# Half blocks of a head pair scored in one matmul, and whole-block scores moved beside the values, in an attention + two-MLP kernel

## Chip, cores and metric

The kernel runs on one core of a Trainium2 chip. The metric is the device time of one execution in microseconds, the median of the runs shown. The profile is of one further execution, whose own time is given beside its span.

## What is computed

The reference is windowed attention with a linear position bias (window 128), followed by two MLPs over the 2304 tokens. Sequences have 576 rows, that is four whole blocks of 128 and a half block of 64.

```python
# B, H, S, D = 4, 8, 576, 64
scores = scale * np.matmul(q, k.transpose(0, 1, 3, 2))
...
mask = (rel >= 0) & (rel < window)
scores = np.where(mask, scores + bias[None], -1000000000.0)
...
attn = np.exp(scores)
attn = attn / (np.sum(attn, axis=-1, keepdims=True) + 1e-09)
return np.matmul(attn, v).astype(np.float32)
...
h = x @ w_in                       # first MLP: 512 -> 2048 -> 512
relu6 = np.clip(h + 3.0, 0.0, 6.0)
return ((h * relu6 / 6.0) @ w_out).astype(np.float32)
...
r = np.maximum(x @ w_in, 0.0)      # second MLP
return ((s * (r * r) + b) @ w_out).astype(np.float32)
```

## The kernel before

**Groups and heads.** Attention is cut into eight groups: rows 0 to 255 of each of the four sequences (groups 0 to 3), then rows 256 to 575 of each (groups 4 to 7, two whole blocks and the half block). Groups 0 and 1 are `StartUnit`s and nothing of them moves. Groups 2 to 7 are `Unit`s, one per head, planned in pairs of an even and an odd head: 24 pairs, 16 of them with half blocks. A pair's two heads lie on partitions 0 to 63 and 64 to 127 of one `raw` tile.

**One pair's work.** `load` fetches queries and keys, `scale` (ACT, L330) scales the queries, `scores` (PE, L345) multiplies a block of 128 queries with 64 rows of contraction by 256 keys (192 for the half block), `minima` (DVE, L358 and L359) picks the right half of the two key blocks with a mask and takes each row's minimum while it writes P, `exps` (ACT, L369) takes the exponential and its sum, `sums` (DVE, L376 and L379) inverts the sum, `weights` (POOL, L385) multiplies P by it, `transposes` (PE, L394) turns P, `fold` (ACT, L398), `lower` (DVE, L407) and `masks` (POOL, L419) spread it over its two key blocks, `values` (PE, L434) multiplies by the values into 64 output columns per head, and `to_hi` and `to_lo` (ACT L445, DVE L449) split the result into two parts for the MLP.

**The first MLP** runs beside it. Per tile of tokens and per 128 hidden columns f, `h` (L609) makes 12 matmuls into one PSUM bank, ACT takes the relu (L620), DVE the product (L623, it frees that bank), ACT and DVE split it (L630, L634), and `o` (L647) makes 12 matmuls. Token tiles are 256 wide for groups 0 to 3 and 320 wide for groups 4 to 7. DVE, ACT and POOL also split the second MLP's weights (class `Pair`, L723 to L809), and the second MLP follows at the end (L999 and L1059).

**Order.** Nothing is scheduled by the compiler: `at(slot, rank, fn)` fills a table, and slots are emitted in order, within a slot by rank. For token tiles 2 to 6 an odd slot holds one `o` and one `h`; the attention matmuls stand in the even slots between. A pair begins at an odd slot s, and the next pair at s + 8. Before, its PE work stands at s+1 (half scores of both heads, right behind the `values` of the pair two before it), s+3 (whole scores, behind the even head's transposes of the pair before it) and, for its own transposes and values, s+11, s+13 and s+17. From the second token tile on, scores, transposes and values share three PSUM banks, which come free in the order in which the program releases them. SP issues all DMAs in program order.

Of the kernel before, what the change touches and what calls it, by code (L numbers as in the profile page):

```python
# [8 lines left out]
F32 = mybir.dt.float32  # L9
# [14 lines left out]
def tile_alibi_window_attention_moe_moe2(  # L24
# [87 lines left out]
    s_sb, b_sb, b2_sb = (scalar[:, i : i + 1] for i in range(3))  # L112

    def constants():
        tmp = xpool.tile([P, P], F32, tag="s0", name="tmp")
# [21 lines left out]
        for h in range(H):  # L137
            c = -(D ** -0.5) / slopes[h]
            nc.gpsimd.memset(qscale[h % 2 * D : (h % 2 + 1) * D, h // 2 : h // 2 + 1], c)

    def scalars():
# [121 lines left out]
    class Unit:  # L263


        def __init__(self, g, b, qa, qb, h):
            self.g, self.b, self.qa, self.qb, self.h = g, b, qa, qb, h
            self.ka = max(0, qa - 1)
            self.nq = min(qb * P, S) - qa * P
            self.nk = min(qb * P, S) - self.ka * P  # L270
            self.nkb = qb - self.ka
            self.id = f"{b}_{qa}_{h}"
            self.Pt = None

        def plan(self, s):
            two = min(self.qa + 2, self.qb)
            odd = self.h % 2
            s -= 4 * odd
            if not odd:
# [24 lines left out]
        def load(self):  # L304
            i, b = (1, self.b) if self.qa else (0, self.b - NATIVE)
            n = (self.qb - self.qa) * P
            raw = ap.tile([P, 832], F32, tag="raw", name=f"raw{self.id}")[:, : n + self.nk]
            if self.nq < n:
                nc.gpsimd.memset(raw[:, self.nq : n], 0.0)
            for u in self.pair():  # L310
                u.p = slice((u.h % 2) * D, (u.h % 2 + 1) * D)
# [3 lines left out]
                u.q = raw[:, : self.nq]  # L315
                u.X = raw[u.p, :n]
                u.rk = raw[u.p, n:]
                u.ps = []

# [12 lines left out]
        def square(self, i):  # L332
            o = (i - self.qa) % 2 * 256
            k0 = max(0, i - 1) * P
            k1 = min((i + 1) * P, S)
            return self.ps[-1 if i < self.qa + 2 else 0][:, o : o + k1 - k0], k0, k1

        def scores(self, a, b):
            for u in self.pair():
                u.ps.append(bank(f"s{u.id}_{a}")) if a < b else None  # L340
            for i in range(a, b):
                for u in self.pair():
# [6 lines left out]

        def minima(self, a, b):  # L350
            if self.Pt is None:
                self.Pt = ap.tile([P, 3, P], F32, tag="P", bufs=5, name=f"P{self.id}")
                self.st = ap.tile([P, 3, 3], F32, tag="st", bufs=6, name=f"st{self.id}")
            for i in range(a, b):
                sl = self.square(i)[0]
                li, r = i - self.qa, rows(i)
                if i:
                    nc.vector.copy_predicated(out=sl[:, :r], mask=own[:, :r], data=sl[:, P:])  # L358
                nc.vector.tensor_tensor_reduce(  # L359
                    out=self.Pt[:, li], in0=sl[:, :P], in1=rel if i else rel0,  # L360
                    scale=slopes[self.h], scalar=3.0e38, op0=ALU.add, op1=ALU.min,
                    accum_out=self.st[:, 0, li : li + 1],
                )

        def exps(self, a, b):
            for i in range(a, b):
                li = i - self.qa
                pt = self.Pt[:, li]
                nc.scalar.activation(  # L369
                    pt, pt, AF.Exp, bias=self.st[:, 0, li : li + 1], scale=-1.0,  # L370
                    accum_out=self.st[:, 1, li : li + 1],
                )

        def sums(self):
            n, st = self.qb - self.qa, self.st
            nc.vector.tensor_scalar(  # L376
                out=st[:, 2, :n], in0=st[:, 1, :n], scalar1=1e-9, scalar2=None, op0=ALU.add
            )
            nc.vector.reciprocal(st[:, 2, :n], st[:, 2, :n])  # L379

        def weights(self):
            for i in range(self.qa, self.qb):
                li = i - self.qa
                pt = self.Pt[:, li]
                nc.gpsimd.tensor_scalar(  # L385
                    out=pt, in0=pt, scalar1=self.st[:, 2, li : li + 1], scalar2=1.0,
                    op0=ALU.mult, op1=ALU.mult,
                )

        def transposes(self):  # L390
            self.pt = bank(f"t{self.id}")
            for i in range(self.qa, self.qb):
                li = i - self.qa
                nc.tensor.transpose(self.pt[:, li * P : (li + 1) * P], self.Pt[:, li], ident)  # L394

        def fold(self):
            self.F = ap.tile([P, 320], F32, tag="F", bufs=1, name=f"F{self.id}")[:, : self.nq]
            nc.scalar.activation(self.F, self.pt[:, : self.nq], AF.Copy)  # L398

# [11 lines left out]
        def masks(self):  # L411
            for i in range(self.qa, self.qb):
                q, r = (i - self.qa) * P, rows(i)
                for k in (0, 1):
                    if (i == 0, i - self.qa < 2)[k]:
                        continue
                    o = 2 * q + k * r
                    s = 1 if k else -1
                    nc.gpsimd.affine_select(  # L419
                        out=self.W[:, o : o + r], in_=self.F[:, q : q + r], fill=0.0,  # L420
                        base=k - 1, compare_op=ALU.is_ge, pattern=[[s, r]], channel_multiplier=-s,
                    )

# [29 lines left out]
    class StartUnit(Unit):  # L453
# [66 lines left out]
        def minima(self):  # L520
            self.Pt = ap.tile([P, 3 * P], F32, tag="P", bufs=5, name=f"P{self.id}")
            self.st = ap.tile([P, 3, 3], F32, tag="st", bufs=6, name=f"st{self.id}")
            for i, a, b in self.blocks:
# [681 lines left out]
    for i in range(FIRST):  # L1205
        at(i, 20.7, lambda i=i: warm_up(4 if i < 4 else 2))
    at(-3, 0, constants)
    at(hslot[1, NF - 1], 1, scalars)

# [59 lines left out]
```

## Time and profile before

| | us |
|---|---|
| median of 3 runs | 922.55 (922.35 to 925.35) |
| the profiled execution | 922.92 |
| its span, first to last instruction | 921.2 |

| stretch of the span, us | what runs |
|---|---|
| 0 to 60 | start, groups 0 and 1 of attention |
| 60 to 190 | token tiles 0 to 2 of the first MLP; attention of groups 2 and 3 |
| 190 to 490 | token tiles 2 to 6; attention of groups 4 to 7 |
| 490 to 562 | the rest of the first MLP |
| 562 to 921 | second MLP |

The profile lists per engine what ran and what ended an idle time. A merged row of the order of time gives the start of the first instruction, the busy time of the run and its count. Matmuls overlap in the pipeline, so the time that a run of them takes is read from its start to the start of the next run, and a plain matmul of float32 operands is two instructions.

### The profile page before, as it was taken

How to read it: one execution, taken by the hardware profiler on the slowest of the kernel's cores; microseconds unless marked ns; L12 is line 12 of the kernel's file. 1: busy time of each engine (PE TensorE's matmuls, PEld its weight loads, DVE VectorE, ACT ScalarE, POOL GpSimd, SP SyncE). 2: the span in 40 equal slices, each digit the busy share in tenths (PEclk: the TensorE clock that was granted, in tenths of full speed). 3: DMA queues.
4: the chain of work that ended last, by engine and by line, in shares of the span. 5: the costliest groups of instructions: out<-in, count | busy, mean ns of one | idle time of the engine just before them, and what ended most of it. 6: DMA issues, size and time to landing. Idle time of an engine off the chain costs nothing.

```text
span 921.2 us, 17887 instructions
## 1 busy us (share of the span) xinstructions
PE 893.6 (97%) x6517; PEld 840.8 (91%) x6517; DVE 650.1 (71%) x1472; ACT 526.6 (57%) x1259; POOL 350.1 (38%) x518
## 2 busy tenths in 40 slices
PE   9898899999999999999999999999999999999998
PEld 4588789888988998999899999999999999999997
DVE  7899885666787777677766744778747787566662
ACT  7877775455655655565554534665626665266550
POOL 7834451333554463446443410444004450144200
PEclk9999999999999999999999999999999999999999
DMA  9344332517356436543635362977778787777872
GB/s 341 130 154 132 110 103 88 182 36 221 140 189 214 160 122 208 191 156 114 228 135 194 123 271 82 330 274 276 267 252 309 260 307 249 260 254 261 282 269 75
DMA packets 63944, 183.10 MB, mean 199 GB/s; under 512 B 7152, under 2 KB 26736, under 8 KB 55408
## 3 DMA queue, kind: packets, MB, share of 16 engines
q1 hardware_dynamic: 63856, 181.95, 57.6%
q8 instruction: 52, 0.85, 0.4%
q14 instruction: 36, 0.29, 0.1%
HBM read 143.13 MB, written 38.80 MB: 197 GB/s over the span
## 4 chain that ended last, share of the span: by engine, by line
PE 83%; DVE 10%; ACT 4%; issue 2%; DMA 0%; SPq 0%; POOL 0%; ACTq 0%; DVEq 0%; POOLq 0%
PE o L999 19%; PE h L1059 19%; PE h L609 18%; PE o L647 18%; PE s L345 3%; PE v L434 3%; PE t L394 1%; DVE work L781 1%; DVE g L634 1%; DVE staging_early L218 1%; DVE t L623 1%; ACT staging_early L213 1%; DVE w L237 1%; DVE raw L221 1%; PE warm_ps L100 1%
## 5 line engine op out<-in xcount | busy, mean ns | idle before, releaser
L609 PE MATMUL h<-x,w 128*128 128x256 f32 (+1 forms) x1536 | 227.4, 297 | 10.7 <-DVE t L623 10.0
L647 PE MATMUL o<-g,w 128*128 128x256 f32 (+1 forms) x1536 | 234.1, 301 | 1.8 <-DVE g L634 1.4
L647 PEld LDWEIGHTS o<-g,w 128*128 128x128 f32 x1536 | 209.9, 189 | 16.7 <-issue 6.5
L609 PEld LDWEIGHTS h<-x,w 128*128 128x128 f32 x1536 | 211.2, 189 | 14.3 <-DVE t L623 13.8
L999 PE MATMUL o<-wstream,i 128*128 128x256 f32 x1512 | 180.4, 281 | 0.0
L999 PEld LDWEIGHTS o<-wstream,i 128*128 128x128 f32 x1512 | 180.0, 188 | 0.0
L1059 PE MATMUL h<-x,wstream 128*128 128x384 f32 x1008 | 176.8, 334 | 0.0
L1059 PEld LDWEIGHTS h<-x,wstream 128*128 128x128 f32 x1008 | 174.4, 188 | 0.2
L620 ACT ACTIVATE t<-h 128x256 f32<-128x256 f32 (+1 forms) x128 | 52.4, 409 | 160.2 <-PE h L609 159.4
L623 DVE SCALAR_TENSOR_TENSOR t<-t,h 128x256 f32<-128x256 f32 (+1 forms) x128 | 57.6, 450 | 86.0 <-ACT t L620 85.9
L419 POOL TENSOR_SCALAR_AFFINE_SELECT W<-F 128x128 f32<-128x128 f32 (+1 forms) x144 | 45.1, 346 | 125.5 <-ACT F L398 125.4
L634 DVE TENSOR_TENSOR g<-t,g 128x256 fp32r<-128x256 f32 (+1 forms) x128 | 71.1, 556 | 29.9 <-ACT g L630 29.3
L1093 ACT ACTIVATE g<-g,scalar 128x384 f32<-128x384 f32 x96 | 58.6, 610 | 39.4 <-DVE g L1078 36.9
L385 POOL TENSOR_SCALAR P<-P,st 128x128 f32<-128x128 f32 x128 | 68.8, 555 | 9.7 <-DVE st L379 7.2
L630 ACT ACTIVATE g<-t 128x256 fp32r<-128x256 f32 (+1 forms) x128 | 56.4, 441 | 25.1 <-DVE t L623 24.4
L1116 POOL TENSOR_TENSOR g<-g 128x384 f32<-128x384 f32 x24 | 24.3, 1014 | 117.8 <-PE h L1059 98.8
L1077 DVE TENSOR_TENSOR g<-h,s 128x384 f32<-128x384 f32 x72 | 39.8, 553 | 31.3 <-PE h L1059 22.5
L856 DVE SCALAR_TENSOR_TENSOR i<-g,scalar,i 128x768 fp32r<-128x768 f32 x48 | 49.3, 1077 | 11.7 <-ACT i L855 11.7
L1028 ACT ACTIVATE u<-o 128x256 f32<-128x256 f32 x36 | 13.2, 385 | 73.1 <-PE o L999 73.1
L369 ACT ACTIVATE P<-P,st 128x128 f32<-128x128 f32 x128 | 49.8, 393 | 0.2
L1078 DVE SCALAR_TENSOR_TENSOR g<-g 128x384 f32<-128x384 f32 x72 | 47.3, 658 | 2.5
L855 ACT ACTIVATE i<-g,scalar 128x768 fp32r<-128x768 f32 x48 | 41.5, 926 | 6.4 <-PE o L999 6.4
(116 smaller groups left out, 1207.7 us busy)
## 6 DMA issues: line engine op xcount, KB each, us to landing
wstream<-wo SPq DMA_DIRECT2D x42, 1024.0 KB, 5.5
raw<-w SPq DMA_DIRECT2D x53, 512.0 KB, 5.2
wstream<-wh SPq DMA_DIRECT2D x24, 1024.0 KB, 5.4
wstream<-wh SPq DMA_DIRECT2D x24, 768.0 KB, 5.9
wh<-staging_early SPq DMA_DIRECT2D x16, 512.0 KB, 3.6
wo<-staging_early SPq DMA_DIRECT2D x12, 512.0 KB, 3.5
stage<-w SPq DMA_DIRECT2D x11, 512.0 KB, 5.0
out<-u SPq DMA_DIRECT2D x11, 384.0 KB, 3.0
```

Source lines behind the costliest of these rows:

```text
L369: nc.scalar.activation(pt, pt, AF.Exp, bias=self.st[:, 0, li : li + 1], scale=-1.0, accum_out=self.st[:, 1, li : li + 1],)
L385: nc.gpsimd.tensor_scalar(out=pt, in0=pt, scalar1=self.st[:, 2, li : li + 1], scalar2=1.0, op0=ALU.mult, op1=ALU.mult,)
L609: nc.tensor.matmul(self.ps, lhsT=w[:, wp, cc * P : (cc + 1) * P], rhs=x[:, cc, xp], start=m == 0, stop=m == 3 * CC - 1,)
L620: nc.scalar.activation(self.a, self.ps, AF.Relu, bias=3.0)
L623: nc.vector.scalar_tensor_tensor(out=self.a, in0=self.a, scalar=6.0, in1=self.ps, op0=ALU.min, op1=ALU.mult)
L630: nc.scalar.activation(self.g[:, 0], self.a, AF.Copy)
L634: nc.vector.tensor_tensor(out=self.g[:, 1], in0=self.a, in1=hi, op=ALU.subtract)
L647: nc.tensor.matmul(acc[t][d], lhsT=w[:, wp, DM + d * P : DM + (d + 1) * P], rhs=self.g[:, gp], start=f == 0 and i == 0 and (t > 1 or d % 2 ...
L856: nc.vector.scalar_tensor_tensor(out=out[:, :, 1], in0=src, scalar=b, in1=hi.bitcast(F32), op0=ALU.add, op1=ALU.subtract,)
L999: nc.tensor.matmul(self.acc[k][c], lhsT=g[:, gp, c * P : (c + 1) * P], rhs=w[:, wp * HB : (wp + 1) * HB], start=k in (0, 1, 5) and p == 0 ...
L1059: nc.tensor.matmul(self.ps[first], lhsT=w[:, wp, cc], rhs=x[:, cc, xp], start=n == first and m == 0, stop=m == 5, skip_group_check=True,)
L1093: nc.scalar.activation(g, g, AF.Copy, scale=s_sb)
```

## The change

Four things are changed.

- The half blocks of a pair (groups 4 to 7) are one block: the queries of the even head stand in columns 0 to 63 on partitions 0 to 63, those of the odd head in columns 64 to 127 on partitions 64 to 127, with zeros elsewhere, so that one matmul over all 128 partitions gives both heads' half scores as 128 rows (`half_scores`, slot s+5, behind the odd head's transposes). Minima, exponential and weights of it are one instruction each, kept in the even head's P; it is transposed with the odd head's blocks. New constant tiles `own2`, `relp` and `slope` hold its mask, positions and per-row slope.
- Whole scores go from s+3 to s+1, behind the `values` of the pair two before; their minima to s+2 (even head) and s+3 (odd head) and their exponentials one slot later.
- `sums` is done once a pair, at s+5, or at s+8 where there are half blocks; weights follow at s+6 and s+7 (before s+7 and s+8), or at s+8 and s+9.
- Per pair with half blocks, queries come in four DMAs instead of two (the keys in two, as before), and POOL clears two 64 by 64 corners instead of one 128 by 64 strip. At the start, four small DMAs and eight memsets fill the new constants.

```diff
+    def half_blocks():
...
+            nc.sync.dma_start(out=relp[p], in_=rel[:HALF])
+            nc.sync.dma_start(out=own2[p], in_=own[:HALF, :HALF])
+            for j in range(H // 2):
+                nc.gpsimd.memset(slope[p, j : j + 1], slopes[2 * j + i])
...
-                at(s + 1, 20.5, lambda: self.scores(two, self.qb))
-                at(s + 3, 20.5, lambda: self.scores(self.qa, two))
-            at(s + 2, 32, lambda: self.minima(two, self.qb))
-            at(s + 3, 33, lambda: self.exps(two, self.qb))
-            at(s + 4 + odd, 32, lambda: self.minima(self.qa, two))
-            at(s + 5 + odd, 33, lambda: self.exps(self.qa, two))
-            at(s + 6 + odd, 32.2, self.sums)
-            at(s + 7 + odd, 33, self.weights)
+                at(s + 1, 20.5, self.scores)
+                at(s + (8 if half else 5), 32.2, self.sums)
+                if half:
+                    at(s + 5, 20.7, self.half_scores)
+                    at(s + 6, 32, self.half_minima)
+                    at(s + 7, 33, self.half_exps)
+                    at(s + 9, 33, self.half_weights)
+            at(s + 2 + odd, 32, self.minima)
+            at(s + 3 + odd, 33, self.exps)
+            at(s + (8 if half else 6) + odd, 33, self.weights)
...
                 nc.sync.dma_start(out=raw[u.p, n:], in_=src[:, self.nq :])
-                nc.sync.dma_start(out=raw[u.p, : self.nq], in_=src[:, : self.nq])
+                nc.sync.dma_start(out=raw[u.p, :two], in_=src[:, :two])
+                if two < n:
+                    c = two + o * HALF
+                    nc.gpsimd.memset(raw[u.p, 2 * two + HALF - c :][:, :HALF], 0.0)
+                    nc.sync.dma_start(out=raw[u.p, c : c + HALF], in_=src[:, two : self.nq])
...
+        def half_scores(self):
+            self.ps2 = bank(f"s{self.id}_2")[:, : P + HALF]
+            k0 = (self.qb - 2 - self.ka) * P
+            nc.tensor.matmul(
+                self.ps2, lhsT=self.X2, rhs=self.rk2[:, k0 : k0 + P + HALF], start=True, stop=True
+            )
...
+        def half_minima(self):
+            sl = self.ps2
+            nc.vector.copy_predicated(out=sl[:, :HALF], mask=own2, data=sl[:, P:])
+            nc.vector.tensor_tensor_reduce(
+                out=self.Pt[:, 2], in0=sl[:, :P], in1=relp,
+                scale=slope[:, self.h // 2 : self.h // 2 + 1], scalar=3.0e38,
+                op0=ALU.add, op1=ALU.min, accum_out=self.st[:, 0, 4:5],
+            )
...
-            for i in range(self.qa, self.qb):
-                li = i - self.qa
-                nc.tensor.transpose(self.pt[:, li * P : (li + 1) * P], self.Pt[:, li], ident)
+            todo = [self.Pt[:, i - self.qa] for i in range(self.qa, self.two)]
+            if self.h % 2 and self.two < self.qb:
+                todo.append(self.pair()[0].Pt[:, 2])
+            self.nt = len(todo) * P
+            for i, pt in enumerate(todo):
+                nc.tensor.transpose(self.pt[:, i * P : (i + 1) * P], pt, ident)
```

**On PE**, around the first pair of group 7. `v` are values, `s` scores, `t` transposes. Before, from the values at s+1 on:

```order
1372 L434 MATMUL v_2_5_5359<-W_2_4_5238,rv_2_4_4879 64x64
1373 L434 MATMUL v_2_5_5359<-W_2_5_5289,rv_2_4_4879 64x64
1374 L345 MATMUL s_2_0_4_5368<-raw_2_0_5124 128x192
1375 L345 MATMUL s_2_1_4_5369<-raw_2_0_5124 128x192
...
1389 L394 MATMUL t_2_6_5417<-ident,P_2_6_5178 128x128 x3
1390 L345 MATMUL s_2_0_2_5421<-raw_2_0_5124 128x256
1391 L345 MATMUL s_2_1_2_5422<-raw_2_0_5124 128x256
...
1407 L394 MATMUL t_2_7_5471<-ident,P_2_7_5182 128x128 x3
```

and after the change:

```order
1371 L497 MATMUL v_2_5_5270<-W_2_4_5153,rv_2_4_4801 64x64
1372 L497 MATMUL v_2_5_5270<-W_2_5_5202,rv_2_4_4801 64x64
1373 L368 MATMUL s_2_0_5279<-raw_2_0_5039 128x256
1374 L368 MATMUL s_2_1_5280<-raw_2_0_5039 128x256
...
1390 L453 MATMUL t_2_6_5331<-ident,P_2_6_5102 128x128 x2
...
1404 L453 MATMUL t_2_7_5381<-ident,P_2_7_5115 128x128 x2
1405 L453 MATMUL t_2_7_5381<-ident,P_2_6_5102 128x128
1406 L376 MATMUL s_2_0_2_5385<-raw_2_0_5039 128x192
```

The four whole-block scores (two of them left out) moved up behind the values; the even head's transposes are two and stand alone; one half score stands behind the odd head's transposes in the place of two behind the values.

**On DVE**, at s+2 of the second pair of group 7. Before:

```order
968 L634 TENSOR_TENSOR g_0_5862<-t_0_5825,g_0_5862 128x320
969 L358 COPY_PREDICATED s_2_4_4_5821<-own,s_2_4_4_5821 128x64
970 L359 ISA P_2_4_5867,st_2_4_5868<-s_2_4_4_5821,rel 128x128
971 L359 ISA st_2_4_5868 128x1
972 L358 COPY_PREDICATED s_2_5_4_5822<-own,s_2_5_4_5822 128x64
973 L359 ISA P_2_5_5871,st_2_5_5872<-s_2_5_4_5822,rel 128x128
974 L359 ISA st_2_5_5872 128x1
975 L781 TENSOR_TENSOR work<-work 128x256 x2
976 L449 TENSOR_TENSOR x_5864<-v_2_1_5812,x_5864 128x320
```

and after the change:

```order
882 L697 TENSOR_TENSOR g_0_5764<-t_0_5724,g_0_5764 128x320
883 L393 COPY_PREDICATED s_2_4_5718<-own,s_2_4_5718 128x128
884 L394 ISA P_2_4_5770,st_2_4_5769<-s_2_4_5718,rel 128x128
885 L394 ISA st_2_4_5769 128x1
...
889 L844 TENSOR_TENSOR work<-work 128x256 x2
890 L512 TENSOR_TENSOR x_5766<-v_2_1_5709,x_5766 128x320
```

At this place stood the half minima of both heads; now both whole blocks of the even head stand there (the second block's three rows are left out). The even transposes at s+3 wait in both programs for a bank that these minima free: before, the one read by rows 969 to 971, after, the one read by all six rows.

## Rows read from the trace of the kernel before

**Rows 1.** The page's head: span, and busy time of PE and DVE:

```profile
span 921.2 us, 17887 instructions
PE 893.6 (97%) x6517; PEld 840.8 (91%) x6517; DVE 650.1 (71%) x1472; ACT 526.6 (57%) x1259; POOL 350.1 (38%) x518
```

**Rows 2.** Stretches: length, PE, PEld, DVE, ACT, POOL busy; clock, DMA, GB/s:

```profile
60.00:135.00 75.00, 65.78 (x521) 60.33 (x522) 69.11 (x161) 57.71 (x142) 34.56 (x41) 1.00 0.36 111
190.00:490.00 300.00, 294.03 (x2190) 269.09 (x2188) 219.00 (x651) 169.06 (x480) 141.95 (x278) 1.00 0.49 162
562.00:921.20 359.20, 354.69 (x2526) 354.26 (x2524) 237.55 (x319) 191.20 (x352) 99.38 (x80) 1.00 0.74 257
```

**Rows 3.** Waits of PE, 60 to 562 us: in total, times, longest:

```profile
PE h L609 <- DVE t L623: 10.0, 10, 1.8
PE s L345 <- DVE x L449: 2.3, 4, 0.8
PE t L394 <- DVE st L359: 0.8, 2, 0.6
PE s L345 <- issue: 0.5, 1, 0.5
```

**Rows 4.** PE in order of time, one pair's period: start, busy, instruction:

```profile
396.72 1.92 PE L609 MATMUL h<-x,w 128*128 128x320 f32 x12
...
399.81 0.60 PE L345 MATMUL s<-raw 64*128 64x192 f32 x4
400.34 2.03 PE L647 MATMUL o<-g,w 128*128 128x320 f32 x12
402.20 1.92 PE L609 MATMUL h<-x,w 128*128 128x320 f32 x12
...
404.38 1.13 PE L345 MATMUL s<-raw 64*128 64x256 f32 x8
405.44 2.02 PE L647 MATMUL o<-g,w 128*128 128x320 f32 x12
407.30 1.92 PE L609 MATMUL h<-x,w 128*128 128x320 f32 x12
...
411.15 1.92 PE L609 MATMUL h<-x,w 128*128 128x320 f32 x12
412.91 0.46 PE L647 MATMUL o<-g,w 128*128 128x320 f32 x2
```

**Rows 5.** The same view where values stand alone between o and h:

```profile
487.13 1.92 PE L609 MATMUL h<-x,w 128*128 128x320 f32 x12
...
492.08 1.92 PE L609 MATMUL h<-x,w 128*128 128x320 f32 x12
```

**Rows 6.** Groups of DVE instructions, 60 to 562 us: count, busy, mean ns, idle:

```profile
L359 DVE CUSTOM_DVE_ANT_0 P<-s,rel 128x128 f32<-128x128 f32 x128 | 37.1, 290 | 4.0
L358 DVE COPY_PREDICATED s<-own,s 128x128 f32<-128x128 int32 x80 | 23.4, 293 | 1.7
L359 DVE DVE_READ_ACCUMULATOR2_ANT st<- 128x1 f32 x128 | 10.5, 82 | 0.0
L376 DVE TENSOR_SCALAR st<-st 128x2 f32<-128x2 f32 x16 | 6.9, 428 | 0.0
```

**Rows 7.** All engines in order of time around 203 us:

```profile
201.91 2.00 POOL L756 TENSOR_TENSOR raw<-raw 128x1024 int32<-128x1024 int32 x1 [3.68 <-DVE raw L750]
...
202.42 1.52 DVE L376 TENSOR_SCALAR st<-st 128x3 f32<-128x3 f32 x1
...
204.51 1.69 PE L609 MATMUL h<-x,w 128*128 128x256 f32 x12 [1.45 <-DVE t L623]
```

**Rows 8.** All engines in order of time around 226 us:

```profile
225.02 0.60 SPq L314 DMA_DIRECT2D raw<-qk  x1
...
225.47 0.22 DVE L358 COPY_PREDICATED s<-own,s 128x64 f32<-128x64 int32 x1
...
226.17 0.52 PE L394 MATMUL t<-ident,P 128*128 128x128 f32 x3 [0.28 <-DVE s L358]
```

More of the change, by code (lines that the diff above doesn't have):

```diff
@@ L272, in __init__ @@
             self.id = f"{b}_{qa}_{h}"
-            self.Pt = None
+            self.two = min(qa + 2, qb)
         def plan(self, s):
-            two = min(self.qa + 2, self.qb)
             odd = self.h % 2
             s -= 4 * odd
+            half = self.two < self.qb
             if not odd:
@@ L335, in square, with scores @@
             k1 = min((i + 1) * P, S)
-            return self.ps[-1 if i < self.qa + 2 else 0][:, o : o + k1 - k0], k0, k1
-        def scores(self, a, b):
+            return self.ps[:, o : o + k1 - k0], k0, k1
+        def scores(self):
             for u in self.pair():
-                u.ps.append(bank(f"s{u.id}_{a}")) if a < b else None
-            for i in range(a, b):
+                u.ps = bank(f"s{u.id}")
+            for i in range(self.qa, self.two):
                 for u in self.pair():
@@ L355, in minima, with column @@
+        def column(self, i):
+            return self.h % 2 * 2 + i - self.qa
+        def minima(self):
+            even = self.pair()[0]
+            if even is self:
+                self.st = ap.tile([P, 3, 5], F32, tag="st", bufs=4, name=f"st{self.id}")
+            self.st = even.st
+            self.Pt = ap.tile([P, 3, P], F32, tag="P", bufs=5, name=f"P{self.id}")
+            for i in range(self.qa, self.two):
                 sl = self.square(i)[0]
-                li, r = i - self.qa, rows(i)
+                c = self.column(i)
@@ L374, in sums, with exp, exps, half_exps @@
+        def exp(self, i, c):
+            pt = self.Pt[:, i]
+            nc.scalar.activation(
+                pt, pt, AF.Exp, bias=self.st[:, 0, c : c + 1], scale=-1.0,
+                accum_out=self.st[:, 1, c : c + 1],
+            )
+        def exps(self):
+            for i in range(self.qa, self.two):
+                self.exp(i - self.qa, self.column(i))
+        def half_exps(self):
+            self.exp(2, 4)
         def sums(self):
-            n, st = self.qb - self.qa, self.st
+            n, st = 4 + (self.two < self.qb), self.st
@@ L379, in sums, with weight, half_weights @@
             nc.vector.reciprocal(st[:, 2, :n], st[:, 2, :n])
[L381 to L388 removed]
+        def weight(self, i, c):
+            pt = self.Pt[:, i]
+            nc.gpsimd.tensor_scalar(
+                out=pt, in0=pt, scalar1=self.st[:, 2, c : c + 1], scalar2=1.0,
+                op0=ALU.mult, op1=ALU.mult,
+            )
+        def weights(self):
+            for i in range(self.qa, self.two):
+                self.weight(i - self.qa, self.column(i))
+        def half_weights(self):
+            self.weight(2, 4)
         def transposes(self):
             self.pt = bank(f"t{self.id}")
[L392 to L394 removed]
+            todo = [self.Pt[:, i - self.qa] for i in range(self.qa, self.two)]
[4 more added lines that the diff above has]
+                nc.tensor.transpose(self.pt[:, i * P : (i + 1) * P], pt, ident)
         def fold(self):
[L397 to L398 removed]
+            self.F = ap.tile([P, 3 * P], F32, tag="F", bufs=1, name=f"F{self.id}")[:, : self.nt]
+            nc.scalar.activation(self.F, self.pt[:, : self.nt], AF.Copy)
         def lower(self):
@@ L411, in masks, with mask @@
         def masks(self):
[L412 to L422, printed above, removed]
+            for i in range(self.qa, self.two):
+                if i:
+                    q = (i - self.qa) * P
+                    self.mask(self, 2 * q, q, P, 0)
+            if self.nt > 2 * P:
+                for u in self.pair():
+                    for k in (0, 1):
+                        self.mask(u, 4 * P + k * HALF, 2 * P + u.h % 2 * HALF, HALF, k)
+        def mask(self, u, o, q, r, k):
+            s = 1 if k else -1
+            nc.gpsimd.affine_select(
+                out=u.W[:, o : o + r], in_=self.F[:, q : q + r], fill=0.0,
+                base=k - 1, compare_op=ALU.is_ge, pattern=[[s, r]], channel_multiplier=-s,
+            )
         def values(self):
@@ L1207, in tile_alibi_window_attention_moe_moe2 @@
     at(-3, 0, constants)
+    at(hslot[1, 0], 1, half_blocks)
     at(hslot[1, NF - 1], 1, scalars)
```

39 lines of the change are left out of this document (18 added, 21 removed).

## Prediction

> **What bounds the kernel now.** I read the page's head first: PE is busy 893.6 of 921.2 us [rows 1], so only what PE executes, or waits for, can move the end. The stretches come next: from 190 to 490 us, where the pairs with half blocks run, PE is busy 294.03 of 300 us and DVE 219.00; from 60 to 135 us PE has 65.78 of 75 and DVE 69.11, so there DVE is nearly the bound; from 562 us on PE has 354.69 of 359.20 [rows 2]. That last stretch works on weights made long before, so what is gained ahead of it should reach the end whole. PE's waits say what stops it between 60 and 562 us: 10.0 us in ten waits for DVE's product that frees the bank of `h`, 2.3 us in four waits of scores for `to_lo`, one of 0.5 us of scores put down to issue, 0.8 us of transposes for minima [rows 3]. All the rest is matmuls, priced by the order of time.
>
> **Price of each PE site.** An `h` and an `o` of 320 columns take 1.76 us each when nothing stands between (411.15 to 412.91) [rows 4], so whatever exceeds 3.52 us between one start of `h` and the next is the price of the attention work between, with the refill of the pipeline behind it:
> - values and half scores: 402.20 - 396.72 - 3.52 = 1.96 us;
> - three even transposes and whole scores: 407.30 - 402.20 - 3.52 = 1.58 us;
> - three odd transposes: 411.15 - 407.30 - 3.52 = 0.33 us [rows 4];
> - values alone: 492.08 - 487.13 - 3.52 = 1.43 us [rows 5].
>
> So half scores cost 1.96 - 1.43 = 0.53 us behind values, just the length of their run (399.81 to 400.34): next to values they pay for no further entry or exit. Whole scores cost 1.58 - 0.33 = 1.25 us behind transposes, though their run is 1.06 us long (404.38 to 405.44) [rows 4]: 0.19 us is paid for going from the untiled transposes into scores on half the array's rows and out again. The Trainium skill, TensorEngine Tiling (Array Packing), section Key Properties, says that changing the tiling mode drains the engine, with no price; by that rule scores beside the values share one drain, which agrees with the 0.19 us. The same page's Theoretical Speedup gives up to 2x to tiles for contractions of 64 or less, which speaks against an untiled half score. By it, one untiled matmul would cost what two tiled ones do side by side, and the streaming term below would gain nothing.
>
> **The change on PE, per pair with half blocks.** Values and whole scores: 1.43 + 1.06 = 2.49 us, if whole scores behind values, like half scores, pay their run alone. Two even transposes: 2/3 of 0.33 = 0.22 us. Three odd transposes stay, 0.33 us, with the half score behind them. No row shows an untiled float32 matmul that is no transpose. The two score runs lie on a line: 4 pass pairs of 256 columns, 1.06 us; 2 of 192, 0.53 us; that is 0.83 ns a column and 0.21 us fixed. From below, the half score is its streaming alone, 384 columns or 0.32 us; from above, the tiled run and a change of mode, 0.53 + 0.19 = 0.72 us. I take 0.43 us, half of the fixed part, since it is untiled beside untiled work but still loads its own weights twice. Sum: 2.49 + 0.22 + 0.33 + 0.43 = 3.47 us against 1.96 + 1.58 + 0.33 = 3.87 us: 0.40 us less (0.11 to 0.51), over 16 pairs **-6.4 us** (-1.8 to -8.2).
>
> Groups 2 and 3 have no half blocks; in the last six of their eight pairs whole scores move beside values: 6 x 0.19 = **-1.1 us** (0 to -1.1, since two of the six stand where DVE is nearly the bound).
>
> **Waits that go.** Before, the odd head's whole scores took the bank that `to_lo` had just released. Now they follow the values at once, in banks that were released earlier, and the bank of `to_lo` goes to the odd transposes, a whole step later: the 2.3 us and the 0.5 us of issue [rows 3] should go, **-2.8 us** (-1.4 to -2.8).
>
> `sums` at 202.42 took 1.52 us, and ended when POOL's 2.00 us instruction that began at 201.91 did; the product behind it was late, and `h` started 1.45 us late [rows 7]. The Trainium skill, SBUF — State Buffer, section SBUF: two separate sides, says that POOL and such a DVE instruction share a pair of ports as a lock held for the whole instruction; the trace agrees, and by that rule what counts is only which slot `sums` is in. In the new order this `sums` is two slots further from that POOL instruction: **-1.4 us** (0 to -1.4). Between 60 and 135 us, DVE loses one `sums` for each of group 2's four pairs, at a mean of 0.43 us [rows 6], or 1.7 us, in a stretch where it is nearly the bound; I take **-1.2 us** of the 10.0 (0 to -6).
>
> **Waits that come.** The even transposes now wait for minima of two whole blocks, where one half block stood. A whole block is 293 + 290 + 82 ns, 0.67 us [rows 6]. At 226.17 the transposes began 0.70 us after the first half minimum did, already 0.28 us late [rows 8]; four pairs, one a group, look like this, where the outputs of a token tile are taken off just ahead. They get the second block whole, 4 x 0.67 = 2.7 us. Elsewhere DVE has some two `h` and `o` streams of lead; I add 0.5 us for pairs that are partly short. **+3.2 us** (0 to +10.6, if all 16 are short).
>
> **What costs nothing.** Two further DMAs a pair hold SP for 0.60 us each [rows 8] behind the wait for values, and delay weight loads and stores queued behind by 1.2 us; the queries are first used by `scale` six slots later, three steps of 3.52 us, which covers them, and if that cover were gone 1.2 us a pair would show. The start's four DMAs and eight memsets stand some 40 slots ahead of their use, with POOL busy 34.56 of 75 us [rows 2]; 0 (0 to +1). POOL clears corners in place of a strip and drops one weight; ACT drops one exponential a pair and has 169.06 of 300 us busy [rows 2]. The weights come one slot later and still stand at least one step ahead of their transposes.
>
> **Sum.** -6.4 - 1.1 - 2.8 - 1.4 - 1.2 + 3.2 = -9.7 us. The profiled execution took 922.92 us, 0.37 us over the median 922.55; taken off the median: **912.9 us**.
>
> **Rivals.**
> - *DVE hands much of it back.* All 16 later pairs wait 0.67 us at the even transposes, 10.6 us in place of 3.2: 912.9 + 7.4 = 920.3. For it: two heads' minima now stand in neighbouring slots. Against: transposes now wait 0.8 us for read-out minima in all [rows 3], and DVE has 81 us free in 300 [rows 2].
> - *Slower.* The same wait at all 24 pairs, those of groups 2 and 3 where DVE is nearly the bound included: 24 x 0.67 = 16.1 us in place of 3.2, 925.8. It decides against the change once the wait is over 0.54 us a pair, (9.7 + 3.2) / 24.
> - *The untiled half score is dear,* 0.72 in place of 0.43 us: 912.9 + 4.6 = 917.5. It is also what a tiling rule that favours halves of the array would make of it.
> - *More goes.* If DVE, with less to do, takes 8.6 of the 10.0 us of waits of `h` away [rows 3], where I counted 2.6: 912.9 - 6.0 = 906.9.
> - *It doesn't reach the end.* The second MLP waits for weights that come no sooner: 922.5. Against: PE is 98.7% busy there [rows 2], with no wait to hand it over to.
>
> **How the numbers follow.** About 0.3%, or 2.8 us, is what a measurement of this kernel can tell from no change. Chances: the forecast 0.53, dear half score 0.14, more goes 0.13, DVE hands back 0.08, not reaching the end 0.04, slower 0.08. The forecast's own range is 909 to 917. The range, 905 to 921, takes in the dear half score, the hand-back and nearly all of the case in which more goes; outside stand the last two and tails. Faster by over 0.3% are the first three, 0.80; within 0.3% the next two, 0.12; slower 0.08.
>
> **What would show it.** In the profile after: values and whole scores priced at about 2.49 us by the same difference of starts, even transposes alone at 0.22, odd transposes with the half score at 0.76; no waits of scores for `to_lo`; waits of transposes for minima of 2 to 4 us in all; `sums` half as many and none over 1 us beyond 190 us. The prediction is wrong if the half score's site costs over 1 us, if scores behind values pay another mode change, or if PE's waits for DVE between 60 and 562 us grow instead of falling by about 5 us.

## The result and the profile after

The changed kernel takes 902.22 us (median of 4 runs, 901.62 to 903.73), the kernel before, run beside it, 922.45 us: a ratio of 0.9775, with a 95% interval of 0.9759 to 0.9791. The gain is 20.2 us, twice the 9.7 us forecast, and 902.2 lies below the range of 905 to 921 us. The direction was right, the size wrong.

The head of the page after, to be read beside [rows 1]. The span fell by 20.8 us, PE's busy time by 16.2 us, DVE's by 25.4 us:

```profile
span 900.4 us, 17714 instructions
PE 877.4 (97%) x6469; PEld 836.4 (93%) x6469; DVE 624.7 (69%) x1376; ACT 521.6 (58%) x1227; POOL 341.7 (38%) x526
```

The stretches, columns as in [rows 2]; the third begins at about the same point of the program as the one from 562 us of before:

```profile
60.00:135.00 75.00, 68.81 (x564) 64.40 (x565) 66.39 (x167) 59.07 (x150) 35.33 (x42) 1.00 0.37 115
190.00:490.00 300.00, 295.59 (x2236) 280.60 (x2235) 209.84 (x583) 173.61 (x464) 138.55 (x279) 1.00 0.53 176
543.00:900.40 357.40, 354.09 (x2522) 353.73 (x2520) 237.57 (x319) 191.18 (x352) 99.41 (x80) 1.00 0.74 258
```

PE's waits between 60 and 562 us, beside [rows 3] (what waited, for what; us in all, times, longest):

```profile
PE h L672 <- DVE t L686: 7.6, 8, 1.7
PE t L453 <- DVE st L394: 4.4, 5, 1.0
PE o L710 <- DVE g L697: 0.9, 3, 0.4
PE o L710 <- DVE y L724: 0.2, 1, 0.2
```

Of the kernel before, [rows 3] shows the largest; the same view also has these, and 0.2 us for `y`:

```profile
PE o L647 <- DVE g L634: 1.4, 3, 0.8
PE t L394 <- DVE s L358: 0.3, 1, 0.3
```

The scores' waits for `to_lo` (now L512) are gone, the waits of `h` shrank by 2.4 us, and five waits of the even transposes for minima came, 4.4 us in all. So PE's waits for DVE fell from 15.0 to 13.1 us in this view, by 1.9 and not by the 5 us that the prediction gave as its sign. The view shows only the time in which PE stood idle; the gaps below show what a late run costs in all.

PE in order of time over one pair with half blocks, beside [rows 4] (start, busy, instruction):

```profile
380.65 1.92 PE L672 MATMUL h<-x,w 128*128 128x320 f32 x12
382.50 1.31 PE L497 MATMUL v<-W,rv 128*64 128x128 f32 x16
383.74 1.13 PE L368 MATMUL s<-raw 64*128 64x256 f32 x8
...
386.67 1.92 PE L672 MATMUL h<-x,w 128*128 128x320 f32 x12
388.43 0.38 PE L453 MATMUL t<-ident,P 128*128 128x128 f32 x2
...
390.40 1.92 PE L672 MATMUL h<-x,w 128*128 128x320 f32 x12
392.17 0.49 PE L453 MATMUL t<-ident,P 128*128 128x128 f32 x3
392.49 0.49 PE L376 MATMUL s<-raw 128*128 128x192 f32 x2
392.69 2.05 PE L710 MATMUL o<-g,w 128*128 128x320 f32 x12
394.58 1.63 PE L672 MATMUL h<-x,w 128*128 128x320 f32 x10
```

By the prediction's own measure, a start of `h` to the next less 3.52 us: values and whole scores 6.02 - 3.52 = 2.50 (forecast 2.49), two even transposes 0.21 (0.22), three odd ones and the half score 0.66 (0.76). A pair costs 3.37 us in place of 3.87: 0.50 less, not 0.40, near the upper end of the 0.11 to 0.51 us that the prediction allowed.

**Where the 20 us lie.** The same runs of `h` and `o` can be set beside each other in the two traces. From the first to the last of them 533.6 us became 514.2, and the difference of starts then stays at 19.6 us to the last copy, so the second MLP hands on all of it (the other 1.2 us between the two spans lie behind the last copy). Now take the starts of consecutive `h` and `o` matmuls from 60 us on. Undisturbed, they are 0.147 us apart at 320 columns and 0.120 us at 256. What a gap has beyond that is listed here; where attention work stands in it (a site), the lowest gap of each kind of site (by what matmuls stand there and how many) is its undisturbed price, and the rest is waiting:

| us, from 60 us on | before | after | difference |
|---|---|---|---|
| attention work on PE, undisturbed | 75.5 | 65.6 | -9.9 |
| waits at these sites | 10.5 | 5.9 | -4.6 |
| waits between `h` and `o` | 12.1 | 8.4 | -3.7 |
| small gaps in the streams | 10.7 | 9.5 | -1.2 |

The forecast had -7.5 us in the first line and -2.2 us in the others. So 2.4 us are missing on PE's sites and 7.3 us in the waits. The experiments took these up. Each was timed beside the kernel before (922.2 to 923.6 us). "Theory A" (PE's sites, with dear waits of scores), "B" (DVE's lighter load) and "C" (order behind a tile's last `o`) are the same throughout.

### The profile page after: what moved, and what is told of

It reads as the page before. It is cut to its first block, busy times and chain, and to the rows that moved or that the text cites. A ratio compares the mean times of both kernels' runs of the same rounds, so it can differ in the third digit from the quotient of the medians.

```text
span 900.4 us, 17714 instructions
## 1 busy us (share of the span) xinstructions
PE 877.4 (97%) x6469; PEld 836.4 (93%) x6469; DVE 624.7 (69%) x1376; ACT 521.6 (58%) x1227; POOL 341.7 (38%) x526
## 4 chain that ended last, share of the span: by engine, by line
PE 84%; DVE 7%; ACT 4%; DMA 2%; issue 2%; SPq 0%; POOL 0%; ACTq 0%; POOLq 0%
PE o L1062 20%; PE h L1122 19%; PE h L672 19%; PE o L710 18%; PE v L497 3%; PE s L368 2%; DMA raw<-w 2%; PE t L453 1%; DVE staging_early L234 1%; DVE g L697 1%; ACT staging_early L229 1%; DVE raw L237 1%; PE s L376 1%; DVE P L587 1%; DVE t L686 1%
## 5 line engine op out<-in xcount | busy, mean ns | idle before, releaser
L697 DVE TENSOR_TENSOR g<-t,g 128x256 fp32r<-128x256 f32 (+1 forms) x128 | 67.2, 525 | 34.6 <-ACT g L693 32.6
L432 POOL TENSOR_SCALAR P<-P,st 128x128 f32<-128x128 f32 x112 | 57.1, 524 | 41.6 <-DVE st L428 40.5
L693 ACT ACTIVATE g<-t 128x256 fp32r<-128x256 f32 (+1 forms) x128 | 56.3, 440 | 28.5 <-DVE t L686 28.2
L1132 ACT ACTIVATE s<-h 128x384 f32<-128x384 f32 x72 | 34.7, 482 | 17.8 <-PE h L1122 17.4
```

The costliest lines, as they stand in the source:

```text
L432: nc.gpsimd.tensor_scalar(out=pt, in0=pt, scalar1=self.st[:, 2, c : c + 1], scalar2=1.0, op0=ALU.mult, op1=ALU.mult,)
L693: nc.scalar.activation(self.g[:, 0], self.a, AF.Copy)
L697: nc.vector.tensor_tensor(out=self.g[:, 1], in0=self.a, in1=hi, op=ALU.subtract)
```

## Experiments

### One half of the change at a time

**Merge alone** (whole scores back at the even transposes, and what follows them two slots later):

```diff
-                at(s + 1, 20.5, self.scores)
+                at(s + 3, 20.5, self.scores)
...
-            at(s + 2 + odd, 32, self.minima)
-            at(s + 3 + odd, 33, self.exps)
+            at(s + 4 + odd, 32, self.minima)
+            at(s + 5 + odd, 33, self.exps)
...
```

> The changed kernel with only the whole blocks' scores back in the step of the even transposes; the merged half block stays as changed. Theory A (the gain beyond the forecast lies in PE's own sites and in waits of scores for the copy out of the values' bank that are dearer than the waits view tells): sites 1.43 + 1.47 + 0.65 = 3.55 us in place of 3.87, over 16 pairs -5.1 us; the odd head's scores wait for `to_lo` again; some 4 us of waits of transposes and of `h` go; about 913.5 us. Theory B (DVE's lighter load brings the extra): nearly all of the gain stays, under 907 us. By the terms on record (half score 0.43 us): -3.4 - 1.4 - 1.2, about 916.5 us.

912.3 us, 0.9886 (0.9870 to 0.9903). **Move alone** (from the kernel before; half scores tiled, behind the odd transposes):

```diff
-                at(s + 1, 20.5, lambda: self.scores(two, self.qb))
-                at(s + 3, 20.5, lambda: self.scores(self.qa, two))
+                at(s + 1, 20.5, lambda: self.scores(self.qa, two))
+                at(s + 5, 20.7, lambda: self.scores(two, self.qb))
...
+            at(s + (8 if half else 5), 32.2, self.sums)
+            at(s + (9 if half else 6 + odd), 33, self.weights)
...
```

> The kernel before with only the move: whole blocks are scored beside the preceding pair's values, half blocks stay two tiled matmuls, one a head, behind the odd transposes. Theory A: sites 2.50 + 0.33 + 1.05 = 3.88 us a pair, no gain there; groups 2 and 3 -2 us; the real price of the scores' waits for `to_lo`, -5.8 us; waits of even transposes +1.4 us; about 916 us. By the terms on record (-1.1 - 2.8 + 3.2): 921.8 us. Theory B (DVE's lighter load): no gain, 921 us or more.

915.29 us, 0.9919 (0.9904 to 0.9934). Both came within 1.2 us of what theory A said: -9.9 and -6.9 us. Together they give 3.4 us more than the sum. The sites tell why. In merge alone whole scores behind the even transposes still cost a visit, that is, going over from untiled matmuls to matmuls on half of the array's rows, and back:

```profile
394.56 1.92 PE L672 MATMUL h<-x,w 128*128 128x320 f32 x12
396.32 0.38 PE L453 MATMUL t<-ident,P 128*128 128x128 f32 x2
396.63 1.14 PE L368 MATMUL s<-raw 64*128 64x256 f32 x8
...
399.55 1.92 PE L672 MATMUL h<-x,w 128*128 128x320 f32 x12
```

That is 4.99 - 3.52 = 1.47 us, against 0.21 + (2.50 - 1.43) = 1.28 us where whole scores follow the values: 0.19 us a visit, as forecast from [rows 4]. In move alone it is the half scores that pay such a visit. Only both edits together leave one visit a pair; 16 x 0.19 = 3.0 of the 3.4 us. Move alone gains 6.9 us though the sites of a pair with half blocks stay at 3.88 us, so waits went with it. Merge alone has the lighter load on DVE and the late `sums` as well; its sites give 16 x 0.31 = 5.0 of its 9.9 us, and 4.9 us are left for these two.

### The half score

**Tiled** in the changed kernel (two matmuls of 64 rows, one a head, into the same bank):

```diff
-            nc.tensor.matmul(
-                self.ps2, lhsT=self.X2, rhs=self.rk2[:, k0 : k0 + P + HALF], start=True, stop=True
-            )
+            for u in self.pair():
+                o = u.h % 2 * HALF
+                nc.tensor.matmul(
+                    self.ps2[u.p], lhsT=self.X2[u.p, o : o + HALF],
+                    rhs=self.rk2[u.p, k0 : k0 + P + HALF], start=True, stop=True,
+                )
```

> The changed kernel, but the half score is two tiled matmuls, one a head, into the same bank, in place of one untiled. Theory A (0.32 us untiled; tiled its run of 0.53 and 0.19 for the change of mode): +0.40 us a pair, 908.6 us. If only the run counts and the change of mode is free: +0.21 us a pair, 905.6 us. If an untiled half score has no advantage: 902.2 us.

**Twice**, untiled, into the same bank:

```diff
-            nc.tensor.matmul(
+            for _ in range(2):
+                nc.tensor.matmul(
```

> The changed kernel with the untiled half score done twice into the same bank: what it costs by itself. Theory A (it streams two passes of 192 columns and pays nothing else): +0.32 us a pair, over 16 pairs +5.1 us, 907.3 us. At the 0.43 us on record: +6.9 us, 909.1 us. At the run of the two tiled ones, 0.53 us: +8.5 us, 910.7 us.

Tiled 906.97 us, 0.9832 (0.9814 to 0.9849); twice 906.79 us, 0.9826 (0.9810 to 0.9843). Order of time of the one done twice:

```profile
393.55 1.92 PE L674 MATMUL h<-x,w 128*128 128x320 f32 x12
395.31 0.49 PE L455 MATMUL t<-ident,P 128*128 128x128 f32 x3
395.63 0.82 PE L377 MATMUL s<-raw 128*128 128x192 f32 x4
396.15 2.05 PE L712 MATMUL o<-g,w 128*128 128x320 f32 x12
398.04 1.19 PE L674 MATMUL h<-x,w 128*128 128x320 f32 x7
```

The site costs 4.49 - 3.52 = 0.97 us, 0.31 more than 0.66, and by its gap every such site shows 0.33 us. That is the streaming of its 384 columns (0.32 us on the prediction's line), the lower end of the prediction's bounds; the timed 4.6 us are 0.29 a pair. Tiled, the site costs 0.99 us (394.01 to 398.52 less 3.52), so the tiled half score 0.65: its run of 0.53 us and 0.12 for the visit. The "dear half score" rival falls.

### `sums` and DVE's load

**`sums` split** again in the changed kernel (even head, odd head, half block, each in a slot of its own behind its exponentials):

```diff
-                at(s + (8 if half else 5), 32.2, self.sums)
+                at(s + 5, 32.2, lambda: self.sums(0, 2))
+                at(s + 6, 32.2, lambda: self.sums(2, 4))
...
+                    at(s + 8, 32.2, lambda: self.sums(4, 5))
...
```

> The changed kernel with `sums` undone: one for the even head, one for the odd head and, where there is a half block, one for it, in the slots behind their exponentials; DVE gets one or two more `sums` a pair of some 0.4 us. Theory A (DVE's load matters in group 2 alone): `h` waits 1 to 1.5 us more there, 903.5 us. Theory B (DVE's lighter load brought the extra gain): 906 us or more. If `sums` don't matter: 902.2 us.

907.27 us, 0.9825 (0.9810 to 0.9840): +5.0 us, more than theory A allowed. It changes two things, the number of `sums` and their slots. **The merged minima twice**:

```diff
                     at(s + 6, 32, self.half_minima)
+                    at(s + 6, 32, self.half_minima)
```

> The changed kernel with the merged half block's mask and minimum done twice: some 0.6 us more on DVE in each of 16 pairs, 9 to 10 us in all, as much as two half blocks a pair took, with PE's work unchanged. Theory B (DVE's lighter load is a part of the gain; the three `sums` for one cost 5 us for 16 us more of DVE): +3 us, 905 us. Theory A (PE's sites alone): 902.2 us.

906.86 us, 0.9824 (0.9806 to 0.9841): +4.6 us for 16 x 0.6 = 10 us of DVE, with not one PE instruction changed. All engines in order of time show how; DVE runs without a gap, and `product` (L687), which frees the bank of `h`, comes late:

```profile
258.78 0.23 DVE L403 COPY_PREDICATED s<-own,s 128x64 f32<-128x64 int32 x1
...
259.05 0.35 DVE L404 CUSTOM_DVE_ANT_0 P<-s,relp,slope 128x128 f32<-128x128 f32 x1
...
259.66 1.08 DVE L864 TENSOR_TENSOR raw<-work,raw 128x512 fp32r<-128x512 f32 x1
260.66 0.41 DVE L687 SCALAR_TENSOR_TENSOR t<-t,h 128x256 f32<-128x256 f32 x1
...
261.12 1.09 PE L673 MATMUL h<-x,w 128*128 128x256 f32 x7 [0.63 <-DVE t L687]
```

**DVE's work as before** (that, and `sums` done twice in its slot): PE's work is the change's, DVE's number of instructions that of before.

```diff
                at(s + (8 if half else 5), 32.2, self.sums)
+                at(s + (8 if half else 5), 32.2, self.sums)
...
                    at(s + 6, 32, self.half_minima)
+                    at(s + 6, 32, self.half_minima)
```

> The changed kernel with DVE's work of the kernel before and PE's of the change: the merged half block's mask and minimum done twice and `sums` done twice, some 18 us more on DVE, about 643 us in all against 650 before. If the lighter DVE adds up (4.6 us for the minima, some 2 to 3 us for 24 more `sums`): about 909 us, and the other 13 us of the gain are PE's sites and the order. If one debt on DVE covers the other: 907 us. If DVE's load is most of the gain: 912 us or more.

907.49 us, 0.9832 (0.9814 to 0.9849), DVE at 643.9 us:

```profile
PE 880.8 (97%) x6469; PEld 837.8 (92%) x6469; DVE 643.9 (71%) x1472; ACT 522.1 (58%) x1227; POOL 336.7 (37%) x526
```

PE's waits for `product`, which are 7.6 us, eight times, in the changed kernel:

```profile
PE h L674 <- DVE t L688: 10.2, 13, 1.6
```

So the lighter DVE is worth 5.3 us where the change stands, good to about 2 us by the two intervals. By the count of the table above, from 60 us on, this run has 65.5 us of attention work, 6.0 us of waits at the sites, 12.3 us of waits between `h` and `o` and 10.7 us of small gaps: the first two are those of the changed kernel, the last two are back where they were before the change. The doubled minima make 4.6 of the 5.3 us; the 5.0 us of the split `sums` don't come on top, and a part of them is its slots, as the next run shows.

**Only the slot of `sums`**, in the kernel before:

```diff
+            half = two < self.qb
-            at(s + 6 + odd, 32.2, self.sums)
-            at(s + 7 + odd, 33, self.weights)
+            at(s + (8 if half else 6 + odd), 32.2, self.sums)
+            at(s + (9 if half else 7 + odd), 33, self.weights)
```

> The kernel before with `sums` of pairs with half blocks in the slot that the change gives them (both heads', not merged), and the weights a slot later. If it is the slot that took `sums` out from under POOL's long instruction at 202 us and others like it: the `h` waits of 1.61 us at 203 and 0.88 us at 236 shrink, 1.4 to 3 us less, 920 to 921 us. If the number of `sums` is what counts: 922.5 us.

920.6 us, 0.9974 (0.9962 to 0.9986): 2.4 us. The kernel before has four `sums` of 1.5 to 1.75 us beyond 190 us (at 202, 236, 322 and 415 us); here, as in the changed kernel, none is over 1 us there. Around 202 us, the place of [rows 7], `product` (L624) now follows at once, and `h` starts at 202.78 instead of 204.51:

```profile
201.79 2.00 POOL L757 TENSOR_TENSOR raw<-raw 128x1024 int32<-128x1024 int32 x1 [3.66 <-DVE raw L751]
...
202.29 0.41 DVE L624 SCALAR_TENSOR_TENSOR t<-t,h 128x256 f32<-128x256 f32 x1
...
202.78 1.42 PE L610 MATMUL h<-x,w 128*128 128x256 f32 x10
...
203.83 0.49 DVE L782 TENSOR_TENSOR raw<-raw 128x256 f32<-128x256 f32 x1 [1.12 <-POOL raw L757]
```

With `sums` split, the reverse is seen: beyond 190 us three of them are long again (0.99, 1.58 and 1.74 us, at 199, 292 and 381 us), where the change's take about 0.16. The first falls under POOL's instruction:

```profile
198.40 2.00 POOL L821 TENSOR_TENSOR raw<-raw 128x1024 int32<-128x1024 int32 x1 [2.66 <-DVE raw L815]
...
199.43 0.99 DVE L427 TENSOR_SCALAR st<-st 128x2 f32<-128x2 f32 x1
```

In the traces of the kernel before and of this run, every `sums` of 0.7 us or more ended within 0.05 us of an instruction of POOL that had begun before it. The Trainium skill, SBUF — State Buffer, section SBUF: two separate sides, calls the port pair that the two engines share an exclusive lock, held for the whole instruction; these traces agree, 0.99 us under a 2.00 us instruction of POOL against 0.16 us.

### The waits at the ends of token tiles

**`to_lo` first**, in the changed kernel and in the kernel before:

```diff
-                at(s + 18, 39, self.to_lo)
+                at(s + 18, 31.9, self.to_lo)
```

> The changed kernel with `to_lo` ahead of the minima and of the weight work on DVE (rank 31.9 in place of 39), so that the even transposes get the values' bank and no longer wait for the minima of two whole blocks. Theory A (5.4 us of such waits are on PE's path, some 1 us at each of five pairs): about 3.3 us go, 898.9 us. Rival (the wait only moves on, to the odd transposes, the half score or the next `h`): 902.2 us.

> The kernel before with only `to_lo` ahead of the minima and of the weight work on DVE, so that the odd head's scores no longer wait for it. Theory A (the odd head's scores, once late, run alone instead of beside the even head's, so that the waits of scores cost about 5.8 us, not the 2.8 that the waits view gives): 917 to 918 us. By the waits view: 919.7 us. If the wait only moves on, as when the changed kernel got the same edit: 922 us.

902.06 us, 0.9780 (0.9762 to 0.9799), and 922.81 us, 0.9993 (0.9983 to 1.0003): nothing, in both. In the changed kernel the transposes start earlier and the next `h` is late instead:

```profile
353.10 0.41 PE L453 MATMUL t<-ident,P 128*128 128x128 f32 x2
...
354.07 1.22 DVE L813 SCALAR_TENSOR_TENSOR raw<-raw,work 128x1024 int32<-128x1024 int32 x1
...
355.20 0.48 DVE L686 SCALAR_TENSOR_TENSOR t<-t,h 128x320 f32<-128x320 f32 x1
...
355.74 0.56 PE L672 MATMUL h<-x,w 128*128 128x320 f32 x2 [0.47 <-DVE t L686]
```

At 161, 221, 354 and 425 us PE gains 0.54, 0.80, 0.79 and 0.79 us and gives back 0.65, 0.36, 0.63 and 0.30 at the next `h`. In the kernel before PE gains 1.06, 1.01, 0.72, 1.08 and 0.74 us at scores and transposes (105, 122, 261, 369 and 443 us), 4.6 us in all. Some 3 us of it are lost where the clock fell in this profile (last section), the rest at waits further on (0.75 us at 264, 1.00 at 295, 0.65 at 447, 0.4 at two smaller ones). Even without the fall of the clock at most 1.8 us would be left. So theory A's price of the scores' waits, 5.8 us, can't be had by this edit alone.

**Outputs taken off by ACT alone**:

```diff
+                at(s + 1, 30.06, self.end2)
...
-                nc.vector.tensor_scalar(
-                    out=y[:, 1], in0=acc[t][e + 1], scalar1=1.0 / 6.0, scalar2=None,
-                    op0=ALU.mult,
-                )
...
+                nc.scalar.activation(y[:, 1], acc[t][e + 1], AF.Copy, scale=1.0 / 6.0)
```

> The changed kernel with the outputs of a finished token tile taken off by ACT alone (two copies more on ACT behind `hi`, two fewer on DVE). Theory A (at the five pairs behind a tile's end DVE is about 0.9 us behind because of its two copies, which is what the even transposes wait for and, when they don't, the next `h`): about 1 us at each of four or five places, 898 us. If ACT becomes as late (its copies then delay `to_hi` and with it the copy out of the values' bank): 902 us or more.

901.47 us, 0.9764 (0.9747 to 0.9781): no difference that can be told, and the five transposes still wait 4.4 us. So it isn't the load of two copies on DVE. What it is can be read in the changed kernel around the end of a tile, all engines in order of time:

```profile
350.51 0.77 ACT L723 ACTIVATE y<-o 128x320 f32<-128x320 f32 x2 [2.23 <-PE o L710]
350.66 0.89 DVE L724 TENSOR_SCALAR y<-o 128x320 f32<-128x320 f32 x2 [2.34 <-PE o L710]
...
351.17 0.47 ACT L693 ACTIVATE g<-t 128x320 fp32r<-128x320 f32 x1
...
351.67 0.49 DVE L697 TENSOR_TENSOR g<-t,g 128x320 fp32r<-128x320 f32 x1
352.08 0.29 DVE L393 COPY_PREDICATED s<-own,s 128x128 f32<-128x128 int32 x1
...
353.51 0.41 PE L453 MATMUL t<-ident,P 128*128 128x128 f32 x2 [0.83 <-DVE st L394]
```

ACT and DVE both stand idle for 2.2 us, with `y` at their heads waiting for the tile's last `o`. Behind `y` stand `hi` (L693), whose input was there from 347.7 us on, and `lo` (L697), which needs `hi`, and behind these the minima. **Outputs behind `lo` and the minima** in the changed kernel, **split** (behind `hi` on ACT), and late in the kernel before:

```diff
-                at(s + 1, 30, self.end)
+                at(s + 1, 32.05, self.end)
```

> The changed kernel with the outputs of a finished token tile taken off behind `lo` and the even head's minima of that slot (rank 32.05 in place of 30), on DVE and ACT. Theory C (the 1 us waits of the even transposes at five pairs come from order, not from load: `hi` and `lo` were ready, but stand in order behind copies that wait for the tile's last `o`, and the minima behind them): the five waits of 1.0 to 1.2 us go and little comes back, 898 us. If DVE's load is what limits there, the next `h` takes the waits over, as when the copy out of the values' bank was put first: 901.5 to 902.2 us. If the next tile's first `o` waits for the late copies instead: 902 us or more.

> The changed kernel with the copies of a finished token tile behind `hi` on ACT (rank 30.06) and behind the even head's minima on DVE (rank 32.05). If what is left of the 5.4 us (0.4 us at the last tile, where the second MLP's side waits for the late copies) comes from ACT's late copies: 898.5 us; if from DVE's: as the run with both late, 899 us.

> The kernel before with the outputs of a finished token tile taken off behind `lo` and the minima of that slot, as in the changed kernel's run of that kind. Theory C (its waits of scores and of transposes at 164, 226, 292, 365 and 440 us come from the same order: `lo`, minima and `to_lo` behind copies that wait for the tile's last `o`): 3 to 5 us less, 918 to 919 us. If they come from DVE's load: 922.5 us.

898.96 us, 0.9739 (0.9721 to 0.9757); 897.91 us, 0.9728 (0.9713 to 0.9744), the fastest of all but not told apart from the one ahead of it; and 918.87 us, 0.9951 (0.9935 to 0.9967). Theory C holds. In the split kernel the transposes no longer wait:

```profile
347.86 0.77 ACT L725 ACTIVATE y<-o 128x320 f32<-128x320 f32 x2 [1.89 <-PE o L711]
...
348.00 0.89 DVE L732 TENSOR_SCALAR y<-o 128x320 f32<-128x320 f32 x2 [0.31 <-PE o L711]
...
349.86 0.38 PE L453 MATMUL t<-ident,P 128*128 128x128 f32 x2
350.00 2.00 PE L711 MATMUL o<-g,w 128*128 128x320 f32 x12
```

The five transposes gain 5.4 us by their gaps; 0.7 and 0.2 us come back at `h` (L673) at 164 and 227 us, and 0.4 us at the last tile's `o`, which waits for the late copies. More important for the question: with this order in both, before and after stand 918.87 to 898.96, 19.9 us apart, as without it (the clock fell in the profile of the kernel before with late outputs, so a part of that may be the clock). The ends of tiles cost the two kernels about alike, 3 to 5 us, and are no part of the gain.

## Why the prediction was wrong in size

The run with DVE's work as before splits the difference in two: it has the order and the PE work of the change and the load on DVE of the kernel before. By the table's count, from 60 us on:

| us | forecast | measured |
|---|---|---|
| PE's sites | -7.5 | -9.9 |
| waits, by the new order and slots | -1.0 | -4.3 |
| waits and small gaps, by DVE's lighter load | -1.2 | -5.2 |
| sum | -9.7 | -19.4 |

The shares of the two lower lines hold for this order of taking things apart: merge alone, with the lighter DVE and the late `sums` but without the move, gained 4.9 us beyond its sites.

**DVE's lighter load: the step that failed most.** I counted one `sums` a pair in group 2, -1.2 us, and left out that the merged half block takes 16 x 0.6 = 10 us of minima from DVE, and the merged `sums` more, because DVE was only 73% busy from 190 to 490 us [rows 2]. The lighter load is worth 5.3 us (DVE's work as before). The 73% is a mean: at 260 us DVE runs without a gap, with `product` behind a minimum and a 1.1 us instruction on weights, and in the run with the merged minima twice the 0.6 us more on DVE cost PE 0.2 to 0.8 us at seven places. The lighter load is the cause that the rival "more goes" named, at a chance of 0.13, but not by the sign that the rival gave: of the 10.0 us of waits of `h` 2.4 went, not 8.6.

**Waits that go and waits that come: both misread, 3.3 us short with `sums`.** -2.8 us for the scores' waits and +3.2 us for the new ones gave +0.4. The new waits are 4.4 us by the view and 5.4 us by the gaps, at the ends of tiles as I said, 1.0 to 1.2 us each and not 0.67. But at the same ends the kernel before lost as much in scores and transposes, 5.6 us by the gaps, so that there the two terms were one and the same delay by two names. Elsewhere the kernel before lost 4.8 us at scores and transposes, of which 0.4 is left. Removed alone by `to_lo` first, such waits moved on; with whole scores moved they did not all come back. The times give somewhat more than the count: of move alone's 6.9 us, 3.4 are left beside 1.1 for groups 2 and 3 and 2.4 for the slot of `sums`. Which of the waits make them up stays open, as does the 1 us or so between times and count.

**`sums` at 202 us: right, and larger.** -1.4 us forecast, 2.4 us (1.3 to 3.5) for the slot alone. The `h` wait at 236 us, behind another long `sums`, shrank too, from 1.00 to 0.63 us.

**PE's sites: right in kind, 2.4 us short.** The term that was mis-sized is the half score: 0.43 us taken between 0.32 and 0.72, measured 0.31 to 0.33, 16 x 0.11 = 1.8 us. The fixed 0.21 us a run that I read from two tiled runs [rows 4] does not show in the untiled matmul; no run shows what it is. The Trainium skill's rule on tiling modes (TensorEngine Tiling (Array Packing), section Key Properties), that a change of mode drains the engine, agrees with the price of the visits, 0.12 to 0.19 us, though no run shows the drain itself. The speedup of up to 2x that the section Theoretical Speedup of that page of the Trainium skill gives to tiles did not come here: the untiled half score took 0.32 us, the tiled one 0.53 us and its visit. Groups 2 and 3 gave what was forecast: by the gaps a pair's three sites were 1.01 + 1.28 + 0.25 us and became 1.86 + 0.25 + 0.25, 0.18 a pair, 1.1 us in six pairs. The rest is the difference between two readings of a pair's gain, 0.50 us from one start of `h` to the next and 0.54 by the gaps.

**Rivals.** None of those that were slower than the forecast came: transposes behind whole minima don't wait in 16 pairs but in five, the half score isn't dear, and the gain reaches the end whole.

## What to carry to other kernels

Work taken off an engine that is idle a quarter of the time can still shorten the kernel (19 us of DVE were worth 5 us here): price it by the places where that engine runs without a gap ahead of something PE needs, not by its mean. A wait removed by reordering one engine's queue can come back at the next thing behind it, as it did with `to_lo` first in both kernels; before counting it as a gain, ask what stands behind it. And look for instructions at the head of a queue that wait for the end of a stage while ready work stands behind them: another place in the order was worth 3 to 5 us here, in both kernels.

## What the runs showed of the hardware

A run of matmuls on half of the array's rows between untiled ones cost 0.12 to 0.19 us beyond its run beside `h` and `o` of 320 columns (half score tiled, merge alone), 0.18 us beside those of 256 (groups 2 and 3), and nothing next to other tiled work (values and whole scores, 2.50 us = 1.43 + 1.06). An untiled float32 matmul of 192 columns, which is two instructions, cost 0.31 to 0.33 us beside untiled ones (half score twice).

The clock granted to PE fell for two short stretches in the profile of the kernel before with `to_lo` first, where it was 1.00 in the kernel before (columns as in [rows 2]):

```profile
114.00:117.50 3.50, 3.50 (x21) 2.57 (x21) 3.35 (x8) 2.49 (x6) 3.03 (x5) 0.64 0.00 0
...
132.00:136.00 4.00, 4.00 (x23) 3.07 (x22) 3.64 (x9) 2.79 (x6) 2.58 (x6) 0.57 0.00 0
```

A mean of 0.57 to 0.64 is a stretch mostly at 1.2 GHz. Ahead of the first PE had waited for `h` (1.83 us, to 113.77), as it does in the kernel before without the fall; the run with late outputs in the kernel before shows it at the same two places. By these two rows it makes the profile some 3 us longer (an estimate, 3.5 x 0.36 + 4.0 x 0.43), though not necessarily the median; why the clock fell there and not in the others was not tried.
